# Two groups of four PSUM banks, and the next expert's transposes moved into the second layer

## The chip, the cores and the metric

The kernel runs on one core of one Trainium2 chip. The metric is the device time of one execution in microseconds (us). The median of three runs before the change is 928.09 us (925.41 to 928.22). TensorE (PE in the profile, PEld for its weight loads) multiplies matrices and writes its results to PSUM, a small memory of eight banks. VectorE (DVE) and ScalarE (ACT) read the results out of the banks; GpSimd (POOL) works on SBUF here, and SyncE (SP) issues most DMAs.

## The reference

Three pieces run one behind the other on 2304 tokens (4 batches of 576) of 512 values.

- Attention with 8 heads of 64, causal, with a window of 128 positions and a linear bias by distance.
- A mixture of eight experts: each token goes to the one expert with the largest gate logit, through `relu(x @ w1[e]) @ w2[e]` (512 to 1024 to 512), and is scaled by its gate probability times a sigmoid.
- A gated layer for all tokens: `silu(x @ w_gate) * (x @ w_val) @ w_out` (512 to 1536 to 512).

```python
for e in range(E):
    h = np.maximum(x[mask] @ w1[e], 0.0)
    out[mask] = gate_w[mask, None] * eom[mask, e, None] * (h @ w2[e])
silu = g * (1.0 / (1.0 + np.exp(-g)))
return (silu * val @ w_out)
```

## The kernel before, in words

**Stages.** Up to about 178 us the attention runs, whose order is written out by hand (`tc.manual_schedule`); it also scatters every token's row, already scaled, into the list of its expert in DRAM (`xs`). From 180 to 447 us the experts run, the fullest first. From 447 us the wide stage, the gated layer, takes the tokens in nine units of 256.

**The order of instructions.** Outside the attention the order on each engine is made by a planner when the kernel is built (`schedule_with_timeline_sim=True`). It goes by its own estimate of times; among instructions that it holds to be ready, those earlier in the program text go first. On the chip each engine then works off its fixed queue, and an instruction that waits holds up all that stand behind it.

**Numbers in two parts.** Every operand of a matmul is split into a high part and the rest that it leaves, and each product is made in three passes (`PASSES`): high by high, high by rest, rest by high. The high part is a copy by ScalarE, the rest a subtraction by VectorE or GpSimd.

**An expert** (loop over `p`) has `caps[p]` rows: 384, 384, 352, 336, 304, 272, 256, 256.

- `load_x(p)` loads its rows from DRAM by a DMA on SP's queue into the only buffer `xr`; `emit_xT(p)` turns them: for each of four blocks of 128 columns, TensorE transposes the rows into a bank `tx` (L907), ScalarE copies it to `xh` (L908) and VectorE makes `xl` (L909).
- First layer: eight groups `m` of 12 matmuls, each into one bank `oh` (L959). ScalarE makes `hh` (relu, L967), VectorE `hl` (L971); with `hl` the bank is free. After each group `w_step(2)` (L972) converts two blocks of weights of later stages.
- Then `emit_xT(p + 1)` and `load_x(p + 2)` (L976, L977).
- Second layer: four banks `oy` are held together. Its eight steps `kk` each take one eighth of the hidden values, `hh[kk]` and `hl[kk]`, into all four banks, 12 matmuls a step (L985). At the end ScalarE copies the banks to `y` (L998) and sends them to DRAM.

**A unit of the wide stage** (loop over `u`) makes 12 groups `m` of 24 matmuls, each into one bank `gv` that holds the gate and the value half (L1019). ScalarE takes the sigmoid (`sg`, L1028), VectorE multiplies (L1029) and makes `av` (L1030), after which the bank is free; ScalarE and VectorE (in unit 0 GpSimd) split `av` into `hh` and `hl`. Then two banks `oo` take the 72 output matmuls (L1043). The weights of this stage come as 64-bit numbers and are narrowed to fp32 by `narrow` (L276 on ScalarE, L277, L278 and L281 on VectorE) before they are split (L328, L329). A third of them is narrowed during the middle experts, the rest from about 406 us to 486 us, beside the last expert and the first unit.

**PSUM before.** All of these results, and the two of the preparation (`cnt_ps`, `warm`), take their banks from one pool of eight under one name, `"m"`, so that the banks go round in the order of the text:

```python
ps_m = wctx.enter_context(tc.tile_pool(name="ps_m", reuse_waits="tile", bufs=8, space=PSUM))
```

For an expert the round is eight `oh`, four `tx`, four `oy`: sixteen, twice all banks. So the four `tx` take the banks of the first four `oh`, the four `oy` those of the last four `oh`, and four of the next expert's eight `oh` those of the `oy`. In the wide stage `gv` of group m takes the bank that `gv` of group m-8 had, but for the two banks that go to `oo` in between.

Of the kernel before, what the change touches and what calls it, by code (L numbers as in the profile page):

```python
# [7 lines left out]
F32 = mybir.dt.float32  # L8
# [10 lines left out]
PSUM = bass.MemoryType.PSUM  # L19
# [7 lines left out]
def attn_moe_glu_kernel(ctx, tc, q, k, v, w_gate, w_ogate, w1, w2, w2_gate, w2_val, w2_out, out, caps=CAPS):  # L27
# [62 lines left out]
    with ExitStack():  # L90
# [35 lines left out]
            load_rows(j - 1, ("vr",))  # L126


        def keep_warm(pool, tag, n):
            o = pool.tile([128, 512], F32, tag=tag, name="warm")  # L130
            for _ in range(n):
                nc.tensor.matmul(out=o, lhsT=ones, rhs=ones.unsqueeze(1).to_broadcast([128, 4, 128]))

# [1 line left out]
        table = ac.tile([128, 1], F32, name="table")  # L135
        nc.scalar.activation(out=table, in_=ones[:, 0:1], func=AF.Exp)
        last_exp = [None]
        keep_warm(ps_t, "t", 12)
        nc.gpsimd.memset(ident, 1.0)
        nc.gpsimd.affine_select(  # L140
            out=ident, in_=ident, pattern=[[-1, 128]], compare_op=ALU.is_equal, fill=0.0, base=0, channel_multiplier=1
# [587 lines left out]
        ht_p = wctx.enter_context(tc.tile_pool(name="ht", reuse_waits="tile", bufs=1))  # L729
        s_p = wctx.enter_context(tc.tile_pool(name="sp", reuse_waits="tile", bufs=2))  # L730
        tb_p = wctx.enter_context(tc.tile_pool(name="tb", reuse_waits="tile", bufs=1))
        ps_m = wctx.enter_context(tc.tile_pool(name="ps_m", reuse_waits="tile", bufs=8, space=PSUM))

        nov = const.tile([128, 1], I32, name="nov")
        oid = const.tile([128, NBLK, 1], I32, name="oid")
        off_reg = [0] * E

        def tb(name, shape, dt=F32):
            return tb_p.tile([128] + shape, dt, tag=name, name=name)
# [10 lines left out]

        def expert_tables():

            cnt_ps = ps_m.tile([128, E], F32, tag="m", name="cnt_ps")
            for i in range(NGR):
                nc.tensor.matmul(out=cnt_ps, lhsT=ones, rhs=gs[:, i, :], start=(i == 0), stop=(i == NGR - 1))
            nc.vector.tensor_copy(cnt[:, 0, :], cnt_ps)
            key, srt = tb("key", [E]), tb("srt", [E])
            STT(out=key, in0=cnt[:, 0, :], scalar=float(E), in1=ktab, op0=ALU.mult, op1=ALU.add)
            nc.vector.max(out=srt, in_=key)
            ki, ci = tb("ki", [E], I32), tb("ci", [E], I32)  # L760
            nc.vector.tensor_copy(ki, srt)
            TS(out=reg[:, 0, :], in0=ki, scalar1=E - 1, scalar2=E - 1, op0=ALU.bitwise_and, op1=ALU.bitwise_xor)
            for p in range(1, E):
                e_reg[p] = nc.sync.value_load(reg[0:1, 0, p:p + 1], min_val=0, max_val=E - 1)
            TS(out=ci, in0=ki, scalar1=(1 << 15) - 1, scalar2=3, op0=ALU.bitwise_and, op1=ALU.logical_shift_right)
            held, end, off, ep = (tb(nm, [1, E]) for nm in ("held", "end", "off", "ep"))
            nc.vector.tensor_copy(ep[:, 0, :], reg[:, 0, :])
            nc.vector.tensor_copy(held[:, 0, :], ci)
            TT(out=held, in0=held, in1=capt, op=ALU.min)
            nc.vector.tensor_copy(end[:, :, 0:1], held[:, :, 0:1])  # L770
            for p in range(1, E):
                TT(out=end[:, :, p:p + 1], in0=end[:, :, p - 1:p], in1=held[:, :, p:p + 1], op=ALU.add)
            nc.vector.tensor_copy(total, end[:, :, E - 1:E])
            TT(out=off, in0=end, in1=held, op=ALU.subtract)
            nc.vector.tensor_copy(reg[:, 1, :], off[:, 0, :])

            own, pick = (t[:, 0:E, :] for t in scratch())
            TT(out=own, in0=iota8.unsqueeze(2).to_broadcast([128, E, E]), in1=ep.to_broadcast([128, E, E]),
               op=ALU.is_equal)
            for src, dst in ((off, offe), (capt, cape)):  # L780
                TT(out=pick, in0=own, in1=src.to_broadcast([128, E, E]), op=ALU.mult)
                RED(out=dst.rearrange("p a e -> p e a"), in_=pick, axis=AX, op=ALU.add)
# [95 lines left out]
        def pair_tile(pool, tag, w):  # L878
            return [pool.tile([128, w], F32R, tag=tag + x, name=tag + x) for x in "hl"]

        def grid(t, n, w):
            return t[:, 0:n * w].rearrange("p (k c) -> p k c", k=n)
# [11 lines left out]
            for x in placed:  # L894
                tc.add_manual_dep(r, x.name, DATA, reason="all tokens are placed")

        def emit_xT(p):
            if p >= E:
                return
            n = caps[p]  # L900
            cb = -(-n // 128)
            r = xr.pop(p)
            xh, xl = (grid(t, KD, n) for t in pair_tile(xe_p, "x", KD * cap))
            for kk in range(KD):
                t = ps_m.tile([128, CP], F32, tag="m", name="tx")
                for c in range(cb):
                    nc.tensor.transpose(t[:, c * 128:c * 128 + 128], r[:, c, kk * 128:kk * 128 + 128], ident)  # L907
                nc.scalar.activation(out=xh[:, kk, :], in_=t[:, 0:n], func=AF.Copy)  # L908
                TT(out=xl[:, kk, :], in0=t[:, 0:n], in1=xh[:, kk, :], op=ALU.subtract)  # L909
            xe[p] = (xh, xl)  # L910

        yr, x2 = {}, {}

# [23 lines left out]
        with tc.issue_after(last_exp[0]):  # L937
            nc.scalar.activation(out=tb("sig", [1]), in_=ident[:, 0:1], func=AF.Sigmoid)
        sorted_known[0] = True
        keep_warm(ps_m, "m", 30)  # L940
        emit_xT(0)
        while wn[0] < 8 or any(w[0][1] == 0 for w in loaded):
            w_step()
        load_x(1)
        for p in range(E):
# [6 lines left out]
                load_order()  # L952
            hh, hl = (grid(t, KF, n) for t in pair_tile(ht_p, "h", HW))
            for m in range(KF):
                o = ps_m.tile([128, cap], F32, tag="m", name="oh")
                i = 0
                for a, b in PASSES:
                    for kk in range(KD):
                        pace[0] = nc.tensor.matmul(  # L959
                            out=o[:, 0:n],  # L960
                            lhsT=wt["w1", p, m // 4, kk][:, a, (m % 4) * 128:(m % 4) * 128 + 128],
                            rhs=(xh, xl)[b][:, kk, :],
                            start=(i == 0),
                            stop=(i == 3 * KD - 1),
                        )
                        i += 1
                r = nc.scalar.activation(out=hh[:, m, :], in_=o[:, 0:n], func=AF.Relu).ins  # L967
                if p == 0 and m > 0:
                    with tc.issue_after(r):
                        off_reg[m] = nc.scalar.value_load(reg[0:1, 1, m:m + 1], min_val=0, max_val=NT)  # L970
                STT(out=hl[:, m, :], in0=o[:, 0:n], scalar=0.0, in1=hh[:, m, :], op0=ALU.max, op1=ALU.subtract)  # L971
                w_step(2)  # L972
                if m % 4 == 3:
                    freed[0] += 2
            if p + 1 < E:
                emit_xT(p + 1)  # L976
                load_x(p + 2)  # L977
            else:

                split_unit(0)  # L980
            o = [ps_m.tile([128, cap], F32, tag="m", name="oy") for _ in range(KD)]
            for kk in range(KF):
                for d in range(KD):
                    for i, (a, b) in enumerate(PASSES):
# [7 lines left out]
                if kk % 2:  # L992
                    freed[0] += 1
                    w_step(2)

            for d in range(KD):
                y = s_p.tile([128, CP], F32, tag="sc", name="y")[:, 0:n]
# [12 lines left out]
        for u in range(NU):  # L1010
            xh, xl = x2.pop(u)
            ah, al = (grid(t, KF2, 256) for t in pair_tile(ht_p, "h", HW))
            for m in range(KF2):
                gv = ps_m.tile([128, 2, 256], F32, tag="m", name="gv")
                for i, nm in enumerate(("g", "v")):
                    n = 0
                    for a, b in PASSES:
# [16 lines left out]
                    out=al[:, m, :], in0=av, in1=ah[:, m, :], op=ALU.subtract  # L1034
                )
            split_unit(u + 1)
            o = [ps_m.tile([128, DM], F32, tag="m", name="oo") for _ in range(2)]

            for kk, c in [(kk, c) for kk in range(KF2) for c in range(2)] if u < NU - 1 else [
                (kk, c) for c in range(2) for kk in range(KF2)  # L1040
# [141 lines left out]
```

## Time and profile before

| | us |
|---|---|
| median of three runs | 928.09 |
| profiled execution | 921.89 |
| its span | 920.0 |
| TensorE matmul busy (share of the span) | 850.5 (92%) |
| VectorE busy | 453.1 (49%) |
| ScalarE busy | 386.7 (42%) |
| GpSimd busy | 319.1 (35%) |

The span is the time from the first to the last instruction of the profiled execution; the 1.9 us around it belong to no instruction. Busy time is an average over stages with different limits: what a change in one stage is worth is read from the waits in that stage. A wait is put down to the engine and line that released it last. A row of the order of time begins with its start and its length; in brackets stands the idle time of the engine before it and what ended it. Matmuls are pipelined, so one is issued before the one ahead of it has ended, and the pace is read from start to start. [...]

### The profile page before, as it was taken

To read this page: it belongs to the slowest core of one execution; us is meant where nothing else is said; L and a number is where in the kernel's file an instruction comes from. 1 tells how busy PE (TensorE), PEld (TensorE's weight loads), DVE (VectorE), ACT (ScalarE), POOL (GpSimd) and SP (SyncE) were. 2 spreads that over 40 slices of the span, in tenths; PEclk is the share of its full clock that TensorE was granted. 3 is DMA by queue.
4 is the path that set the end of the run, shared out by engine and by line. 5 is a ranking of instruction groups with operands and counts; after the bars stand their busy time and mean duration, and the time that the engine had idled before them with its cause. 6 is when DMAs were issued, how large, how long until landed. Compare 5 with 4: busy or idle time off the path is not lost.

```text
span 920.0 us, 17155 instructions
## 1 busy us (share of the span) xinstructions
PE 850.5 (92%) x6291; PEld 781.3 (85%) x6291; DVE 453.1 (49%) x1292; ACT 386.7 (42%) x1046; POOL 319.1 (35%) x395
## 2 busy tenths in 40 slices
PE   7995987599699989998989999999999999999995
PEld 5784765399599989998988989999898989899994
DVE  6774899582454563249994423324141424233240
ACT  6894875152455656566663212223121212122220
POOL 4673876343156788775563000000000000000000
PEclk9997999889899999999999999999999999999998
DMA  9999521579766677666650101010100001010000
GB/s 186 206 297 256 151 70 40 171 169 130 209 200 203 205 232 241 208 187 201 199 175 2 46 1 46 1 47 1 47 1 27 20 1 47 1 47 1 25 1 25
DMA packets 105370, 99.36 MB, mean 108 GB/s; under 512 B 62786, under 2 KB 71490, under 8 KB 105282
## 3 DMA queue, kind: packets, MB, share of 16 engines
q1 hardware_dynamic: 95952, 83.47, 34.7%
q0 software_dynamic: 3520, 9.50, 2.8%
q10 hardware_dynamic: 5810, 5.25, 1.7%
q8 instruction: 51, 0.84, 0.4%
q14 instruction: 37, 0.30, 0.1%
HBM read 77.16 MB, written 21.04 MB: 107 GB/s over the span
## 4 chain that ended last, share of the span: by engine, by line
issue 29%; PE 28%; DVE 4%; POOL 2%; DMA 1%; ACT 0%; POOLq 0%; DVEq 0%; ACTq 0%
PE gv L1019 12%; PE oo L1043 7%; PE oy L985 5%; PE oh L959 4%; DVE rawd L277 1%; DVE rawd L278 1%; POOL out_dram L1053 1%; DVE rawd L281 1%; POOL w L329 1%; DMA ys<-y 0%; DMA rawd<-in_moe_w_gate_dram 0%; DMA rawd<-in_moe_w_val_dram 0%; POOL hl L1033 0%; PE tx L907 0%; DVE hl L971 0%
## 5 line engine op out<-in xcount | busy, mean ns | idle before, releaser
L1053 POOL DMA_INDIRECT out_dram<-xr,oid x18 | 17.3, 962 | 398.6 <-ACT xr L1052 388.7
L1029 DVE TENSOR_TENSOR sg<-gv,sg 128x256 f32<-128x256 f32 x108 | 45.8, 424 | 222.7 <-ACT sg L1028 222.7
L1043 PE MATMUL oo<-w,hh 128*128 128x512 f32 x432 | 137.8, 396 | 0.9 <-DVE av L1030 0.9
L1019 PE MATMUL gv<-xh,w 128*128 128x256 f32 x864 | 126.6, 281 | 3.3 <-DVE av L1030 3.3
L985 PE MATMUL oy<-hh,w 128*128 128x384 f32 (+5 forms) x512 | 119.0, 319 | 11.2 <-DVE hl L971 11.1
L1019 PE MATMUL gv<-xh,wx 128*128 128x256 f32 x864 | 125.0, 279 | 0.0
L1019 PEld LDWEIGHTS gv<-xh,w 128*128 128x128 f32 x864 | 112.9, 189 | 3.8 <-DVE av L1030 3.8
L1019 PEld LDWEIGHTS gv<-xh,wx 128*128 128x128 f32 x864 | 112.4, 188 | 0.7
L323 POOL TENSOR_TENSOR w<-raw,w 128x512 fp32r<-128x512 f32 x80 | 103.7, 1323 | 26.0 <-ACT w L321 14.5
L985 PEld LDWEIGHTS oy<-hh,w 128*128 128x128 f32 x512 | 89.6, 196 | 13.6 <-DVE hl L971 13.6
L321 ACT ACTIVATE w<-raw 128x512 fp32r<-128x512 f32 x128 | 74.5, 624 | 58.7 <-DMA raw<-in_moe_w_dram 39.4
L1043 PEld LDWEIGHTS oo<-w,hh 128*128 128x128 f32 x432 | 81.3, 188 | 20.5 <-DVE av L1030 1.3
L959 PE MATMUL oh<-xh,w 128*128 128x384 f32 (+5 forms) x512 | 91.5, 318 | 7.0 <-ACT y L998 5.5
L1028 ACT ACTIVATE sg<-gv 128x256 f32<-128x256 f32 x108 | 41.3, 382 | 112.2 <-PE gv L1019 111.9
L959 PEld LDWEIGHTS oh<-xh,w 128*128 128x128 f32 x512 | 81.3, 195 | 8.0 <-ACT y L998 6.0
L1043 PE MATMUL oo<-w,hl 128*128 128x512 f32 x216 | 85.4, 396 | 0.0
L1031 ACT ACTIVATE hh<-av 128x256 fp32r<-128x256 f32 x108 | 45.1, 418 | 92.6 <-DVE av L1030 92.4
L985 PE MATMUL oy<-hl,w 128*128 128x384 f32 (+5 forms) x256 | 81.0, 317 | 0.0
L1019 PE MATMUL gv<-xl,w 128*128 128x256 f32 x432 | 68.7, 281 | 0.0
L1019 PE MATMUL gv<-xl,wx 128*128 128x256 f32 x432 | 68.3, 279 | 0.0
L1033 DVE TENSOR_TENSOR hl<-av,hh 128x256 fp32r<-128x256 f32 x98 | 41.6, 425 | 44.1 <-ACT hh L1031 44.1
L1052 ACT ACTIVATE xr<-oo 128x512 f32<-128x512 f32 x18 | 10.8, 598 | 120.1 <-PE oo L1043 119.3
(201 smaller groups left out, 1478.7 us busy)
## 6 DMA issues: line engine op xcount, KB each, us to landing
raw<-in_moe_w_dram SPq DMA_DIRECT2D x128, 256.0 KB, 3.5
xs<-zrow SPq DMA_DIRECT2D x8, 774.0 KB, 7.2
rawd<-in_moe_w_gate_dram SPq DMA_DIRECT2D x24, 256.0 KB, 3.1
rawd<-in_moe_w_val_dram SPq DMA_DIRECT2D x24, 256.0 KB, 2.9
rawd<-in_moe_w_out_dram SPq DMA_DIRECT2D x24, 256.0 KB, 3.1
xr<-xs SPq DMA_DIRECT2D x6, 774.0 KB, 6.5
xr<-ys SPq DMA_DIRECT2D x9, 512.0 KB, 3.8
qr<-in_q_dram SPq DMA_DIRECT2D x16, 256.0 KB, 4.9
```

Source lines behind the costliest of these rows:

```text
L321: nc.scalar.activation(out=s[:, 0, :], in_=t, func=AF.Copy)
L323: low = lambda: eng.tensor_tensor(out=s[:, 1, :], in0=t, in1=s[:, 0, :], op=ALU.subtract)
L959: pace[0] = nc.tensor.matmul(out=o[:, 0:n], lhsT=wt["w1", p, m // 4, kk][:, a, (m % 4) * 128:(m % 4) * 128 + 128], rhs=(xh, xl)[b][:, kk, ...
L985: pace[0] = nc.tensor.matmul(out=o[d][:, 0:n], lhsT=wt["w2", p, 0, kk][:, a, d * 128:d * 128 + 128], rhs=(hh, hl)[b][:, kk, :], start=(kk ...
L1019: nc.tensor.matmul(out=gv[:, i, :], lhsT=wt[nm, -1, m // 4, kk][:, a, (m % 4) * 128:(m % 4) * 128 + 128], rhs=(xh, xl)[b][:, kk, :], start ...
L1028: nc.scalar.activation(out=sg, in_=gv[:, 0, :], func=AF.Sigmoid)
L1029: TT(out=sg, in0=gv[:, 0, :], in1=sg, op=ALU.mult)
L1031: nc.scalar.activation(out=ah[:, m, :], in_=av, func=AF.Copy)
L1033: (nc.gpsimd if u == 0 and m < 10 else nc.vector).tensor_tensor(out=al[:, m, :], in0=av, in1=ah[:, m, :], op=ALU.subtract)
L1043: nc.tensor.matmul(out=o[c], lhsT=(ah, al)[b][:, kk, c * 128:c * 128 + 128], rhs=wt["o", -1, 0, kk][:, a, :], start=(kk == 0 and i == 0), ...
L1052: nc.scalar.activation(out=ob[:, c, :], in_=o[c], func=AF.Copy)
L1053: r = nc.gpsimd.indirect_dma_start(out=out[:, :], out_offset=bass.IndirectOffsetOnAxis(ap=oid[:, 2 * u + c, :], axis=0), in_=ob[:, c, :], ...
```

## The change

The pool `ps_m` gets two names, `"oh"` and `"oy"`, of four buffers each, in place of one name of eight. To `"oh"` go the counts, the warm-up, the first layer, the transposes and `gv`; to `"oy"` the second layer, `oo` and the transposes of the first expert. `emit_xT(p + 1)` and `load_x(p + 2)` move from between the two layers to behind the first of the eight steps of the second layer (`kk == 0`). `keep_warm` gets its number of buffers as an argument; the number is the pool's own in both calls.

```diff
-        ps_m = wctx.enter_context(tc.tile_pool(name="ps_m", reuse_waits="tile", bufs=8, space=PSUM))
+        ps_m = wctx.enter_context(tc.tile_pool(name="ps_m", reuse_waits="tile", bufs=1, space=PSUM))
...
+        def bank(tag, w, name):
+            return ps_m.tile([128, w], F32, tag=tag, name=name, bufs=4)
...
-            cnt_ps = ps_m.tile([128, E], F32, tag="m", name="cnt_ps")
+            cnt_ps = bank("oh", E, "cnt_ps")
...
-        def emit_xT(p):
+        def emit_xT(p, tag="oh"):
...
-                t = ps_m.tile([128, CP], F32, tag="m", name="tx")
+                t = bank(tag, CP, "tx")
...
-        keep_warm(ps_m, "m", 30)
-        emit_xT(0)
+        keep_warm(ps_m, "oh", 30, 4)
+        emit_xT(0, "oy")
...
-                o = ps_m.tile([128, cap], F32, tag="m", name="oh")
+                o = bank("oh", cap, "oh")
...
-            if p + 1 < E:
-                emit_xT(p + 1)
-                load_x(p + 2)
-            else:
+            if p + 1 == E:
                 split_unit(0)
-            o = [ps_m.tile([128, cap], F32, tag="m", name="oy") for _ in range(KD)]
+            o = [bank("oy", cap, "oy") for _ in range(KD)]
             for kk in range(KF):
...
                 if kk % 2:
                     freed[0] += 1
                     w_step(2)
+                elif kk == 0:
+                    emit_xT(p + 1)
+                    load_x(p + 2)
...
-                gv = ps_m.tile([128, 2, 256], F32, tag="m", name="gv")
+                gv = bank("oh", 512, "gv").rearrange("p (a c) -> p a c", a=2)
...
-            o = [ps_m.tile([128, DM], F32, tag="m", name="oo") for _ in range(2)]
+            o = [bank("oy", DM, "oo") for _ in range(2)]
```

## Rows read from the trace of the kernel before

**Rows 1.** Page, part 1: busy us (share of the span) and instructions of each engine.
```profile
PE 850.5 (92%) x6291; PEld 781.3 (85%) x6291; DVE 453.1 (49%) x1292; ACT 386.7 (42%) x1046; POOL 319.1 (35%) x395
```

**Rows 2.** Waits of PE: line, released by, us in total, times, longest.
```profile
PE oy L985 <- DVE hl L971: 11.1, 8, 3.2
...
PE oh L959 <- ACT y L998: 5.5, 2, 4.5
...
PE gv L1019 <- DVE av L1030: 3.3, 2, 3.1
```

**Rows 3.** Windows: stretch, length, busy PE, PEld, DVE, ACT, POOL, PEclk, DMA, GB/s.
```profile
523.00:862.00 339.00, 339.00 (x2386) 316.13 (x2385) 107.64 (x242) 77.57 (x177) 13.41 (x14) 1.00 0.06 20
...
432.00:440.00 8.00, 5.86 (x34) 5.66 (x35) 8.00 (x21) 5.00 (x14) 4.14 (x5) 0.79 0.66 218
...
465.00:475.00 10.00, 10.00 (x86) 9.85 (x84) 10.00 (x24) 6.04 (x17) 6.28 (x8) 1.00 0.70 230
475.00:486.00 11.00, 7.65 (x50) 7.39 (x50) 10.55 (x23) 6.00 (x17) 8.28 (x11) 0.85 0.16 48
```

**Rows 4.** Order of time on PE, wide unit 0: start us, length us, instruction, wait.
```profile
446.63 0.63 PE L1019 MATMUL gv<-xh,wx 128*128 128x256 f32 x4
447.10 0.63 PE L1019 MATMUL gv<-xl,wx 128*128 128x256 f32 x4
...
481.50 0.74 PE L1019 MATMUL gv<-xh,w 128*128 128x256 f32 x4 [3.15 <-DVE av L1030]
...
485.80 0.59 PE L1043 MATMUL oo<-w,hh 128*128 128x512 f32 x1
...
503.94 0.28 PE L1019 MATMUL gv<-xh,wx 128*128 128x256 f32 x1
```

**Rows 5.** Order of time on DVE, wide unit 0: the first six `av`.
```profile
465.00 0.41 DVE L1030 TENSOR_TENSOR av<-gv,sg 128x256 f32<-128x256 f32 x1
...
469.41 0.41 DVE L1030 TENSOR_TENSOR av<-gv,sg 128x256 f32<-128x256 f32 x1
...
474.79 0.42 DVE L1030 TENSOR_TENSOR av<-gv,sg 128x256 f32<-128x256 f32 x1
...
481.04 0.41 DVE L1030 TENSOR_TENSOR av<-gv,sg 128x256 f32<-128x256 f32 x1
...
485.14 0.41 DVE L1030 TENSOR_TENSOR av<-gv,sg 128x256 f32<-128x256 f32 x1
...
487.25 0.43 DVE L1030 TENSOR_TENSOR av<-gv,sg 128x256 f32<-128x256 f32 x1 [0.52 <-POOL hl L1033]
```

**Rows 6.** Order of time on PE, experts 1 to 3.
```profile
221.48 0.86 PE L959 MATMUL oh<-xh,w 128*128 128x384 f32 x4
222.17 0.86 PE L959 MATMUL oh<-xl,w 128*128 128x384 f32 x4
...
238.61 1.65 PE L959 MATMUL oh<-xh,w 128*128 128x384 f32 x4 [4.48 <-ACT y L998]
...
270.93 0.81 PE L959 MATMUL oh<-xh,w 128*128 128x352 f32 x4
...
304.81 0.77 PE L959 MATMUL oh<-xh,w 128*128 128x336 f32 x4
305.42 0.78 PE L959 MATMUL oh<-xl,w 128*128 128x336 f32 x4
...
319.68 1.47 PE L907 MATMUL tx<-ident,xr 128*128 128x128 f32 x12
...
328.93 0.49 PE L985 MATMUL oy<-hh,w 128*128 128x336 f32 x1 [3.21 <-DVE hl L971]
```

**Rows 7.** Order of time on DVE: first `hl` of expert 1, first and last of expert 3.
```profile
242.13 0.55 DVE L971 SCALAR_TENSOR_TENSOR hl<-oh,hh 128x384 fp32r<-128x384 f32 x1
...
313.94 0.51 DVE L971 SCALAR_TENSOR_TENSOR hl<-oh,hh 128x336 fp32r<-128x336 f32 x1 [3.84 <-ACT hh L967]
...
328.38 0.49 DVE L971 SCALAR_TENSOR_TENSOR hl<-oh,hh 128x336 fp32r<-128x336 f32 x1
```

More of the change, by code (lines that the diff above doesn't have):

```diff
@@ L126, in attn_moe_glu_kernel, with keep_warm @@
             load_rows(j - 1, ("vr",))
-        def keep_warm(pool, tag, n):
-            o = pool.tile([128, 512], F32, tag=tag, name="warm")
+        def keep_warm(pool, tag, n, bufs):
+            o = pool.tile([128, 512], F32, tag=tag, name="warm", bufs=bufs)
             for _ in range(n):
@@ L137, in attn_moe_glu_kernel @@
         last_exp = [None]
-        keep_warm(ps_t, "t", 12)
+        keep_warm(ps_t, "t", 12, 3)
         nc.gpsimd.memset(ident, 1.0)
@@ L901, in emit_xT @@
             cb = -(-n // 128)
-            r = xr.pop(p)
-            xh, xl = (grid(t, KD, n) for t in pair_tile(xe_p, "x", KD * cap))
+            xe[p] = xh, xl = [grid(t, KD, n) for t in pair_tile(xe_p, "x", KD * cap)]
             for kk in range(KD):
-                t = ps_m.tile([128, CP], F32, tag="m", name="tx")
+                t = bank(tag, CP, "tx")
                 for c in range(cb):
-                    nc.tensor.transpose(t[:, c * 128:c * 128 + 128], r[:, c, kk * 128:kk * 128 + 128], ident)
+                    nc.tensor.transpose(
+                        t[:, c * 128:c * 128 + 128], xr[p][:, c, kk * 128:kk * 128 + 128], ident
+                    )
                 nc.scalar.activation(out=xh[:, kk, :], in_=t[:, 0:n], func=AF.Copy)
                 TT(out=xl[:, kk, :], in0=t[:, 0:n], in1=xh[:, kk, :], op=ALU.subtract)
-            xe[p] = (xh, xl)
         yr, x2 = {}, {}
```

## The prediction

> **What bounds the kernel now.** I read the busy shares first, then who TensorE waits for, then the stages by windows, and last the order of time around each wait. TensorE is busy for 850.5 of 920.0 us [rows 1], and from 523 to 862 us it is busy for 339.00 of 339.00 [rows 3]: units 1 to 7 of the wide stage are TensorE alone, and nothing that touches only the other engines can be seen there. What an edit can win or lose lies in the places where TensorE stands. In the two stages that the change touches these are four [rows 2]: the second layer of an expert (`oy`) waits 11.1 us in 8 places for the vector engine's `hl` (L971), the first layer (`oh`) 5.5 us for the copies of the results `y` (L998), the wide stage (`gv`) 3.3 us for `av` (L1030). So at most about 20 us can be removed, and the bank that a group of matmuls writes to is what ties it to these engines. The reader is to see in the windows that in unit 0 of the wide stage it is the vector engine that sets the pace: 10.00 of 10.00 us from 465 to 475, 10.55 of 11.00 from 475 to 486 [rows 3], because it still converts the last wide weights there (L277, L278, L281). Only there does TensorE run far ahead of those that empty its banks.
>
> **The change, part by part.** Instructions are the same in kind and number: the same transposes, copies, subtractions and DMAs; `keep_warm` gets the same three buffers as before. What changes is which bank each result takes, and where the transposes of the next expert stand. So every term is a wait.
>
> *Wide stage, unit 0: four banks for `gv` in place of eight.* Of today's eight banks the first group `gv0` starts at 446.63 and four matmuls take 0.47 us (446.63 to 447.10), so a group of 24 takes 2.82 [rows 4]. A bank is free when `av` has read it: `av0` ends at 465.00 + 0.41 = 465.41, `av1` at 469.82, `av2` at 475.21, `av3` at 481.45, `av4` at 485.55, `av5` at 487.68 [rows 5]. With eight banks TensorE meets this only at the eleventh and twelfth group: `gv11` starts at 481.50 after 3.15 us of waiting, when `av3` is through, and the output matmuls `oo` start at 485.80 [rows 4]. With four banks group m waits for `av` of m-4. If the vector engine keeps its order and pace, `gv4` starts at 465.4 instead of 446.63 + 4 x 2.82 = 457.9; `gv5` at 469.8, `gv6` at 475.2, `gv7` at 481.5, `gv8` at 485.6. From there TensorE is the slower one again (2.82 a group, while `av4` to `av5` is 2.1): `gv9`, `gv10`, `gv11` follow without a wait, and `oo` starts at 485.6 + 4 x 2.82 = 496.9. That is 11.1 us later than 485.80. Given back: `oo` today takes 503.94 - 485.80 = 18.1 us [rows 4] with some waiting in it for `av`; without it I take 1 us off (estimate; between 0 and 1.4). Term: +10 us. Its lower end is 0: if the evacuations stood earlier in the vector engine's queue, the conversions of the output weights, which `oo` needs only after 486, could wait. I take the upper value, since the queues are fixed when the kernel is built and an evacuation becomes ready only when its group is done, which four banks make no earlier. Queued behind a waiting `gv` are only more `gv` and `oo`; the vector engine has its conversions to do meanwhile. In the later units TensorE has no wait at all [rows 3], so four banks do as well as eight: 0.
>
> *First layer, four banks for `oh`.* The same rule: group m waits for `hl` of m-4. In expert 1 a group of 12 takes 3 x 0.69 = 2.08 us (221.48 to 222.17 for four), so the fifth would start at 221.48 + 8.3 = 229.8, while `hl0` ends at 242.13 + 0.55 = 242.68 [rows 6, 7]. Today TensorE stands from 234 to 238.61 for `y` [rows 6] and then three more times for `hl` at the second layer's banks. After, it stands once, 12.9 us, and does four groups from 242.7 to 251.0, or to 253 at the lower clock of the first ones; the second layer then finds free banks and runs its 8 x 2.08 = 16.6 us and the transposes' 1.5, to 269 or 271. Today expert 2 begins at 270.93 [rows 6]. Term: 0, between -2 and +2.
>
> *Second layer, banks of its own; transposes behind its first eighth.* Expert 3 shows the exchange best. `hl0` ends at 314.45 [rows 7], the fifth group of 1.86 us each (304.81 to 305.42 for four) would start at 312.25: +2.2. Today's first layer ends at 319.68, where the transposes start; after it ends at 314.45 + 4 x 1.86 = 321.9. Then the first eighth runs at once, since its banks are free, and the wait of 3.21 us at 328.93 [rows 6], which is for the bank of the last `hl` (328.38 + 0.49), goes from `oy` to the last of the four transposes, which now take the `oh` banks; by then two or three eighths are done. Today's 3.2 and the slow matmuls behind it go, 2.2 and a rest of the wait come: I take -2, between -3.5 and +1. Transposes, their 12 matmuls in some 1.5 us [rows 6], cost the same in either place. Behind them stand the copies `xh`, `xl` and SP's load of the rows of the expert after next; all are moved by one eighth, about 2 us, with seven eighths (13 us) left before the next first layer needs them. That cover hides them; it is gone only if the last `hl` is later than the whole second layer. SP's weight loads queued behind that row load would then wait too: up to +2 in an expert. Experts 2 and 7 have waits of the same sort of 1 to 2 us, which turn from one bank's wait into another's: 0, between -2 and +1. The other experts have hardly any wait now, 8 for `hl` and 2 for `y` in all [rows 2]: 0.
>
> The sum: +10 (unit 0) + 0 (expert 1) - 2 (expert 3) + 0 = +8 us. The profiled execution took 921.9 us, 920.0 of span and 1.9 around it; after, about 930. The runs shown (925.4 to 928.2, median 928.1) all lie above it, the median by 6 us; the difference is what carries over, so I add the 8 to the median: 936.
>
> [...]
>
> **Rivals.**
> 1. *The clock stays low through the bank waits.* Five waits in 30 us, and then `gv8` to `gv11` at 4.30 us instead of 2.82: 4 x 1.48 = +6 on top, 942. For it: the windows of 0.79 and 0.85. Against it: `gv8` hardly waits, since `gv7` ends when `av4` does. Chance 0.15.
> 2. *The queues come out in another order, and the bank waits of unit 0 vanish (faster).* The planner lays the queues anew. If it puts `av0` to `av4` some 10 us earlier among the conversions, term one is 0, and what is left is what the second layer wins: -2 by expert 3, up to -6 if experts 1, 2 and 7 keep a third of their waits off; taking the middle, 924. It decides from `av4` ending before 475. Against it: the vector engine is full up to 486, and its conversions come from weights that TensorE's progress frees, not from the banks. Chance 0.15.
> 3. *Both halves meet:* part of the evacuations move, unit 0 loses 2 to 4 us, the experts win as much; 928. That is also where a change that only renames banks would stand. Chance 0.15.
>
> **How the numbers follow.** The forecast has 0.55, with its own range of 931 to 940 (+3 to +12: the bounds of expert 1, expert 3 and of the give-back in `oo`). The range to hold the time 8 times in 10 takes in most of rivals 1 and 3 and leaves out half of rival 2: 926 to 943. What a measurement of this kernel can tell from no change is 0.3%, 2.8 us. Faster by more: 0.14 (rival 2, without its end near nothing). Within: 0.16 (rival 3 and the edge of rival 2). Slower: 0.70 (forecast and rival 1).
>
> **What would show it.** In the profile after: TensorE's waits of `gv` for `av` grow from 3.3 us to some 15, in about five places, the first near `gv4`; `oo` of unit 0 starts some 8 to 11 us later, counted from `gv0`. `oy` for `hl` falls from 11.1 to under 4, some of it back under the transposes (`tx`); `oh` for `y` is replaced by one wait of over 10 us for `hl` in expert 1. Units 1 to 7 keep their length to 0.1%. The prediction is wrong if `gv` does not wait more than now, or if the stage of the experts gains over 6 us.

## The result and the profile after

The changed kernel takes 935.7 us, the median of four runs (931.6 to 939.9); the kernel before took 927.5 in four runs beside them (925.4 to 928.2). By the medians that is 8.2 us slower. The ratio of the runs is 1.0102 with a 95% interval of 1.0061 to 1.0143, or 9.5 us slower, between 5.7 and 13.3. The forecast was 936. The profiled execution took 933.1 us, its span 931.1, against 921.9 and 920.0.

Busy time is nearly what it was [rows 1], so the time went into waits:

```profile
PE 852.7 (92%) x6291; PEld 782.5 (84%) x6291; DVE 460.6 (49%) x1292; ACT 386.6 (42%) x1046; POOL 320.8 (34%) x395
```

The waits of TensorE after the change (released by, us in total, times, longest). The 11.1 us of `oy` for `hl` [rows 2] are gone; `oh` and the transposes `tx` wait for `hl` instead, and `gv` waits 9.0 us where it waited 3.3:

```profile
PE oh L963 <- DVE hl L975: 10.5, 3, 8.5
PE gv L1023 <- DVE av L1034: 9.0, 3, 6.4
...
PE tx L910 <- DVE hl L975: 4.9, 2, 2.5
PE oy L986 <- ACT hh L971: 4.3, 1, 4.3
```

Unit 0 of the wide stage in TensorE's order of time, to set against [rows 4]. Read the starts: the first four groups take 2.82 us each, `gv4` waits 6.40 us (468.20) for `av0`, two later groups wait less. From 488.42, where `gv8` begins, four groups take 11.3 us without a wait, so each is at its full pace. Eight of the 72 matmuls of `oo` stand in the gaps from 480.10 on; the other 64 begin at 499.74, and unit 1 at 514.68:

```profile
450.34 0.63 PE L1023 MATMUL gv<-xh,wx 128*128 128x256 f32 x4
...
468.20 1.22 PE L1023 MATMUL gv<-xh,wx 128*128 128x256 f32 x4 [6.40 <-DVE av L1034]
...
473.39 0.63 PE L1023 MATMUL gv<-xh,wx 128*128 128x256 f32 x4
...
477.17 0.74 PE L1023 MATMUL gv<-xh,wx 128*128 128x256 f32 x4 [0.79 <-DVE av L1034]
...
480.10 0.40 PE L1047 MATMUL oo<-w,hh 128*128 128x512 f32 x1
...
483.02 0.85 PE L1023 MATMUL gv<-xh,wx 128*128 128x256 f32 x4 [1.82 <-DVE av L1034]
...
488.42 0.66 PE L1023 MATMUL gv<-xh,w 128*128 128x256 f32 x4
...
499.74 0.63 PE L1047 MATMUL oo<-w,hh 128*128 128x512 f32 x2
...
514.68 0.28 PE L1023 MATMUL gv<-xh,wx 128*128 128x256 f32 x1
```

The first and the fifth `av` of that unit on the vector engine. They lie 17.4 and 37.5 us behind `gv0`; before it was 18.4 and 38.5 [rows 4, 5]. All of the first five end 1.0 to 2.2 us earlier than before by this count. So the evacuations (the reads that empty the banks) kept about their place and pace:

```profile
467.74 0.41 DVE L1034 TENSOR_TENSOR av<-gv,sg 128x256 f32<-128x256 f32 x1
...
487.86 0.41 DVE L1034 TENSOR_TENSOR av<-gv,sg 128x256 f32<-128x256 f32 x1
```

Windows (length; busy PE, PEld, DVE, ACT, POOL; PEclk, DMA, GB/s). PEclk is the mean clock that was granted to TensorE, as a share of full speed. The first begins with the transfers of the last 48 wide-weight chunks (a chunk is the block of 128x256 weights that is narrowed and split at a time), in expert 6, and ends with the last copy of one (L328): the vector engine is idle for 7.1 of 85.0 us. The last is units 1 to 7, TensorE alone as in [rows 3]; each of these units takes 50.72 us in both kernels:

```profile
403.87:488.90 85.03, 69.44 (x521) 67.43 (x521) 77.94 (x170) 48.55 (x135) 53.55 (x57) 0.90 0.58 177
459.00:468.00 9.00, 2.80 (x24) 2.60 (x23) 9.00 (x19) 5.27 (x15) 5.45 (x7) 0.91 0.84 239
468.00:475.00 7.00, 6.80 (x38) 6.80 (x39) 7.00 (x15) 4.36 (x13) 4.77 (x6) 0.63 0.64 220
565.00:918.00 353.00, 353.00 (x2513) 330.06 (x2512) 113.86 (x258) 81.84 (x189) 14.37 (x15) 1.00 0.06 21
```

The same stretch before (both begin 9 us behind expert 6's first `oh`) has 2.6 us of idle time in 81.7:

```profile
403.56:485.30 81.74, 75.14 (x603) 73.85 (x603) 79.14 (x170) 49.27 (x133) 51.48 (x57) 0.96 0.60 183
```

What makes the vector engine idle can be seen on GpSimd. A group of the second half-copies of the wide weights (L329), its duration in ns (least, median, most), from expert 6 to the end of unit 0, first before and then after:

```profile
L329 POOL TENSOR_TENSOR w<-rawd,w x48: 739/872/1798, 412.9 to 485.8; 128x256 fp32r<-128x256 f32 x48
```

```profile
L329 POOL TENSOR_TENSOR w<-rawd,w x48: 737/834/3874, 413.6 to 490.1; 128x256 fp32r<-128x256 f32 x48
```

After the change one copy lasts 3.87 us, and while it lasts the vector engine works through its conversions without a gap, at 0.28 and 0.42 us each. The buffers that this copy and the four behind it hold come free late, the transfers into them start late (the longest wait of a transfer for such a copy, from 405 to 430 us, grows from 2.2 to 5.5 us), and the vector engine stands for 3.32 us. SP's waits for these copies (in total, times, longest), before and after; then GpSimd's row, and the vector engine's last rows of that run and the first after the gap:

```profile
SPq L302 <- POOL w L329: 9.8, 11, 2.2
```

```profile
SPq L302 <- POOL w L329: 11.0, 9, 5.5
```

```profile
417.42 3.87 POOL L329 TENSOR_TENSOR w<-rawd,w 128x256 fp32r<-128x256 f32 x1 [2.05 <-ACT w L328]
```

```profile
419.73 0.29 DVE L277 TENSOR_SCALAR rawd<-rawd 128x256 int32<-128x256 int32 x1
419.93 0.75 DVE L278 SCALAR_TENSOR_TENSOR rawd<-rawd 128x256 int32<-128x256 int32 x2
424.01 0.30 DVE L277 TENSOR_SCALAR rawd<-rawd 128x256 int32<-128x256 int32 x1 [3.32 <-DMA rawd<-in_moe_w_gate_dram]
```

### The profile page after: what moved, and what is told of

The parts are those of the page before. It is cut to its first block, busy times and chain, and to the rows that moved or that the text cites. A ratio compares the mean times of both kernels' runs of the same rounds, so it can differ in the third digit from the quotient of the medians.

```text
span 931.1 us, 17143 instructions
## 1 busy us (share of the span) xinstructions
PE 852.7 (92%) x6291; PEld 782.5 (84%) x6291; DVE 460.6 (49%) x1292; ACT 386.6 (42%) x1046; POOL 320.8 (34%) x395
## 4 chain that ended last, share of the span: by engine, by line
PE 36%; issue 32%; DMA 9%; DVE 8%; POOL 8%; ACT 5%; SPq 1%; POOLq 0%; DVEq 0%; ACTq 0%
PE gv L1023 13%; PE oo L1047 7%; PE oh L963 6%; PE oy L986 4%; DMA raw<-in_moe_w_dram 4%; POOL w L323 3%; DMA rawd<-in_moe_w_gate_dram 2%; PE s L360 2%; DMA rawd<-in_moe_w_val_dram 2%; ACT p L402 1%; PE o L451 1%; DVE w L323 1%; POOL w L329 1%; PE tq L344 1%; POOL out_dram L1057 1%
## 5 line engine op out<-in xcount | busy, mean ns | idle before, releaser
L1023 PE MATMUL gv<-xh,wx 128*128 128x256 f32 x864 | 127.1, 282 | 9.0 <-DVE av L1034 9.0
L1023 PEld LDWEIGHTS gv<-xh,wx 128*128 128x128 f32 x864 | 113.7, 190 | 10.6 <-DVE av L1034 9.9
L986 PE MATMUL oy<-hh,w 128*128 128x384 f32 (+5 forms) x512 | 116.8, 313 | 5.1 <-ACT hh L971 4.3
L963 PE MATMUL oh<-xh,w 128*128 128x384 f32 (+5 forms) x512 | 93.4, 321 | 13.0 <-DVE hl L975 10.5
L321 ACT ACTIVATE w<-raw 128x512 fp32r<-128x512 f32 x128 | 76.1, 627 | 64.1 <-DMA raw<-in_moe_w_dram 39.7
L986 PEld LDWEIGHTS oy<-hh,w 128*128 128x128 f32 x512 | 87.1, 191 | 5.8 <-ACT hh L971 4.5
```

The lines of the kernel that those rows point to most:

```text
L321: nc.scalar.activation(out=s[:, 0, :], in_=t, func=AF.Copy)
L963: pace[0] = nc.tensor.matmul(out=o[:, 0:n], lhsT=wt["w1", p, m // 4, kk][:, a, (m % 4) * 128:(m % 4) * 128 + 128], rhs=(xh, xl)[b][:, kk, ...
L986: pace[0] = nc.tensor.matmul(out=o[d][:, 0:n], lhsT=wt["w2", p, 0, kk][:, a, d * 128:d * 128 + 128], rhs=(hh, hl)[b][:, kk, :], start=(kk ...
L1023: nc.tensor.matmul(out=gv[:, i, :], lhsT=wt[nm, -1, m // 4, kk][:, a, (m % 4) * 128:(m % 4) * 128 + 128], rhs=(xh, xl)[b][:, kk, :], start ...
```

## The experiments

One table carries them. It cuts each profile at four points: A, the first `oh` of expert 6; B, the last L328 copy of a wide weight; C, the first `gv` of unit 1; and the end. From C to the end it is 416.1 to 416.5 us in every kernel of the table. A itself scatters by 10 us between executions of the same queues, so the stretches are compared and not the profiles' totals. The stretches scatter too: e2 and e10 have the same queues from A on, and differ by 3.3 us from A to `gv0` and by 1.3 from A to C. In e6, e7, e9 and e12 the last copy stands later by design, so only A to C can be compared there. Ratios are to the kernel before on the same chip; "long copies" are GpSimd copies of 128x256 over 2 us near there.

| kernel | median us | ratio (95%) | A to gv0 | A to B | B to C | A to C | long copies |
|---|---|---|---|---|---|---|---|
| before | 927.5 | | 52.1 | 90.7 | 18.7 | 109.4 | none |
| after | 935.7 | 1.0102 (1.0061–1.0143) | 55.5 | 94.0 | 25.8 | 119.8 | 3.87 |
| e1 banks alone | 936.9 | 1.0075 (1.0048–1.0103) | 53.5 | 92.7 | 25.3 | 118.0 | 4.01 |
| e2 move alone | 930.9 | 1.0028 (1.0010–1.0046) | 55.6 | 96.1 | 18.7 | 114.7 | 3.89, 2.47 |
| e3 gv in turn | 935.6 | 1.0062 (1.0041–1.0084) | 56.7 | 93.7 | 24.1 | 117.8 | 3.88 |
| e4 and expert 7 | 935.3 | 1.0062 (1.0043–1.0081) | 57.8 | 94.8 | 23.7 | 118.6 | 3.88 |
| e5 gv in rounds | 931.4 | 1.0027 (1.0006–1.0047) | 55.7 | 93.8 | 19.5 | 113.2 | 3.88 |
| e6 chunks behind av | 925.5 | 0.9949 (0.9931–0.9967) | 52.0 | 98.6 | 9.0 | 107.6 | none |
| e7 e5 and e6 | 926.9 | 0.9967 (0.9953–0.9980) | 55.5 | 98.8 | 9.1 | 107.9 | 3.88 |
| e8 shift only | 916.8 | 0.9853 (0.9826–0.9881) | 48.1 | 66.9 | 39.7 | 106.6 | none |
| e9 last rows back | 925.8 | 0.9976 (0.9957–0.9996) | 54.8 | 100.0 | 9.1 | 109.1 | 4.01 |
| e10 last rows alone | 931.0 | 1.0024 (1.0004–1.0043) | 52.3 | 94.7 | 18.7 | 113.4 | 3.88, 2.47 |
| e12 four banks, e6 | 935.1 | 1.0087 (1.0072–1.0102) | 55.2 | 98.6 | 16.6 | 115.2 | 3.88 |

So the profiled 11.1 us between before and after are: +0.3 up to A, +3.3 from A to B, +7.1 from B to C, +0.4 behind C.

**e1, the banks alone.** The changed kernel with the transposes put back:

```
-            if p + 1 == E:
+            if p + 1 < E:
+                emit_xT(p + 1)
+                load_x(p + 2)
+            else:
                 split_unit(0)
...
-                elif kk == 0:
-                    emit_xT(p + 1)
-                    load_x(p + 2)
```

> Only the bank half of the change: two groups of four, with the transposes back between the two layers. Theory T (the time goes to the wait for a bank wherever the vector engine lags: 7.0 us in unit 0 of the wide stage, 3.4 us in expert 7): 8 to 11 us above the kernel before, within 2 us of the changed kernel; unit 0 from its first gv to unit 1's first gv takes 63 to 65 us against 57.3 before. Rival R (the transposes in their new place move the order of the queues, and that costs it): within 3 us of the kernel before, unit 0 at 57 to 59 us.

Measured: +7.0 us (4.5 to 9.6 by the interval), unit 0 in 64.5 us. Theory T holds for unit 0; the move isn't needed for most of the loss. Of T's 3.4 us in expert 7 only 1.4 show (A to `gv0`).

**e2, the move alone.** The kernel before with its eight banks, and `emit_xT(p + 1)`, `load_x(p + 2)` behind `kk == 0`.

> Only the other half: eight banks under one tag as before, the next expert's transposes behind kk = 0 of the second layer. Theory T: within 2 us of the kernel before, unit 0 at 57 to 58 us; in the experts the first-layer tiles of the next expert now take banks that the second layer's results left last, so a wait of 2 to 5 us before the first layer of one or two experts can stand in the trace and make it up to 4 us slower. Rival R: at least 6 of the changed kernel's 8 us appear here.

Measured: +2.6 us (0.9 to 4.3), B to C 18.7 as before. The two halves, 7.0 and 2.6, make 9.6; the whole, 8.2, has that in its interval. That is above T's 2 us, within the 4 that it allowed for waits in the experts, and far from R's 6. Unit 0's length came out at 59.1, above what T said: its first five `av` ended 1.0 to 1.9 us later behind `gv0`, and there were two long copies (3.89 and 2.47 us) on GpSimd.

**e3, gv over both groups in turn.**

```
-                gv = bank("oh", 512, "gv")...
+                gv = bank(("oh", "oy")[m % 2], 512, "gv")...
```

> The changed kernel, with the wide stage's gv tiles taken from the two groups in turn, so that eight are open again; experts as changed. Theory T: unit 0 back to 57 to 58.5 us from 64.35, the total 6 to 7 us under the changed kernel (929 to 930 by medians), expert 7's 3 us stay. Rival R (the order of the queues, not the number of open banks): within 2 us of the changed kernel, unit 0 above 62 us.

Measured: 935.6 us, 5.8 above the kernel before (3.8 to 7.8), B to C 24.1 against the changed kernel's 25.8, unit 0 in 61.1. T as I had put it, eight open banks are enough, is wrong: no `gv` waits for an `av` any more, but `oo` does. The rows of TensorE:

```profile
496.02 0.76 PE L1047 MATMUL oo<-w,hh 128*128 128x512 f32 x1 [4.31 <-DVE av L1034]
...
499.35 0.79 PE L1047 MATMUL oo<-w,hh 128*128 128x512 f32 x1 [1.71 <-DVE av L1034]
```

With the groups in turn the two `oo` tiles take the banks of `gv5` and `gv7`, in the kernel before those of `gv4` and `gv5`. Behind the wait the clock is low too (0.57 in this window):

```profile
496.00:507.00 11.00, 9.27 (x24) 6.84 (x25) 6.29 (x14) 5.40 (x14) 3.75 (x6) 0.57 0.00 1
```

**e4, expert 7's `oh` in turn as well** (`bank("oy" if p == E - 1 and m % 2 else "oh", ...)`).

> As the kernel with eight open gv tiles, and expert 7's first-layer tiles also taken from the two groups in turn. Theory T: the wide stage begins at 446 to 448 us again instead of 450.3 and the total is 9 to 11 us under the changed kernel by the profiles, so within 2 us of the kernel before. A second explanation for expert 7 (its conversions were late because a transfer of wide weights was issued 1.7 us later, with 4.3 us of gap on the vector and scalar engines near 424 us, not because of banks): the wide stage still begins at 449 to 451 us and the total stays within 1 us of the kernel with eight gv tiles alone.

Measured: as e3 (935.3 and 935.6), and A to `gv0` is 57.8. More banks for `oh` in expert 7 give nothing, so its 3.4 us are not a matter of how many `oh` has. That leaves the late transfers, which e9 and e10 test.

**e5, gv in rounds of eight.** `bank("oh" if m % 8 < 4 else "oy", ...)`, so that every tile of unit 0 meets the same `av` as with one group of eight.

> The changed kernel with the wide stage's gv tiles in rounds of eight: m 0 to 3 and 8 to 11 from the first group, 4 to 7 from the second, so that the two oo tiles take the banks of gv4 and gv5, as in the kernel before (with the groups in turn they took those of gv5 and gv7, free at 495.9 and 499.3 us). Theory T2 (unit 0's part of the cost is which av each bank waits for): from the start of the last wide-weight copy on the scalar engine (L328) to unit 1's first gv it takes 18.6 to 19.5 us, as before and with the move alone (18.6 both), against 25.8 in the changed kernel and 24.1 with the groups in turn; total 929 to 932 us. What is left above the kernel before, 1 to 3 us, is the held copy on GpSimd (3.9 us near 420 us). Rival (any second group of banks costs it): still 24 to 26 us and a total of 935 to 937 us.

Measured: B to C 19.5 us, total +2.5 (0.6 to 4.4). Against the changed kernel's ratio that takes back 7 us with one line. Unit 0's term is which `av` a bank waits for. What is left is as large as the move alone.

**e6, the chunks of the output weights behind the `av`s**, on the kernel before. `tc.issue_after(r)` keeps what stands under it, as far as it runs on the engine of `r`, behind `r` in that engine's queue:

```
-        while wjobs or loaded:
+        while any(w[0][0] != "o" for w in wjobs + loaded):
             w_step()
+        w_step(4)
...
-                TT(out=av, in0=gv[:, 1, :], in1=sg, op=ALU.mult)
+                r = TT(out=av, in0=gv[:, 1, :], in1=sg, op=ALU.mult).ins
+                with tc.issue_after(r):
+                    w_step(2)
```

> The kernel before, with all but the first four chunks of the output weights converted behind unit 0's av's, two behind each, instead of ahead of them. Theory T2 (in unit 0 the vector engine is the bound, and which of its work comes first decides what TensorE waits for): av0 ends at about 452 to 456 us instead of 465, no gv waits, oo runs close behind the last chunk, and unit 1 begins 2 to 5 us earlier counted from gv0: unit 0 takes 52 to 56 us against 57.3; total 924 to 927 us by medians of the kernel before's 929. Rival (the vector engine's whole work bounds unit 0 whatever its order): unit 0 at 57 to 59 us, total within 1.5 us of the kernel before.

Measured: 925.5 us, 4.7 us under the kernel before (3.1 to 6.4), the fastest median here; unit 0 takes 55.6 and no `gv` waits. A to C is 107.6 against 109.4 (110.4 in e11, which has the kernel before's queues up to C). So 1.8 to 2.7 of the 4.7 us lie there; where the rest lies these profiles don't show. One step of T2 missed: `av0` was to end 5 to 9 us behind `gv0` and ended 17.4 behind it (before, 18.8). It is the next ones that came earlier: `av1` to `av5` end 20.4 to 35.5 us behind `gv0`, before 23.2 to 41.0.

**e7, e5 and e6 together** on the changed kernel.

> The changed kernel with both edits: gv tiles in rounds of eight, and the output weights' chunks behind the av's. Theory T2: as the kernel before with the chunks behind the av's, plus 1 to 3 us for the held copy on GpSimd: unit 0 at 52 to 56 us, total 925 to 930 us. Rival: at or above 930 us, unit 0 above 57 us.

Measured: 926.9 us, 3.1 under the kernel before (1.9 to 4.4). TensorE is busy for 51.57 of unit 0's 52.45 us. The intervals of e6, e7 and e9 overlap; which is fastest isn't settled:

```profile
453.06:505.51 52.45, 51.57 (x363) 47.12 (x361) 45.11 (x95) 27.64 (x76) 27.95 (x36) 1.00 0.40 121
```

**e8, two of the three vector operations of a conversion left out** (L278 and L281), on the changed kernel.

> The changed kernel with two of the vector engine's three operations on each of the 72 wide-weight chunks left out (the two that put the bits together; what it computes there is not the reference's). Theory T (four banks cost only where the vector engine lags behind TensorE): unit 0 takes 50.7 to 53 us and no gv waits over 1 us for an av; the total is 20 to 35 us under the changed kernel. Rival (four banks, or the order of the queues, cost by themselves): unit 0 stays above 57 us, with waits of gv.

Measured: 916.8 us, 13.7 under the kernel before and so some 20 under the changed one, but unit 0 takes 58.5 us, and `gv4` still waits:

```profile
457.73 1.22 PE L1017 MATMUL gv<-xh,wx 128*128 128x256 f32 x4 [6.08 <-DVE av L1028]
```

Theory T's 50.7 to 53 us without waits are refuted, and the rival's signs came: over 57 us, with waits of `gv`. The rival left open whether banks or the order of the queues cost it; the trace points to the order. The vector engine isn't full there; from 440 to 458 us it waits 13 times for transfers, at the shift of the next chunk, and `av0` stands behind those shifts in its queue:

```profile
DVE rawd L277 <- DMA rawd<-in_moe_w_out_dram: 7.1, 13, 1.5
```

So the lag that four banks are too few for is one of place in the queue and not only of load. That is also what e6 uses. No GpSimd copy of 128x256 over 2 us stands here, where the vector engine's runs are thin (those 13 waits make 7.1 us).

**e9, the last expert's transposes alone put back**, on e7 (`elif kk == 0 and p + 2 != E`, and the old place for `p + 2 == E`).

> The changed kernel with gv in rounds of eight and the output weights' chunks behind the av's, and with the transposes of the last expert alone put back between the layers of expert 6. Theory T3 (expert 7's 3.4 us come from the last expert's transposes in their new place: the vector engine then runs without a stop near 418 us, a GpSimd copy lasts 3.9 us instead of 0.9, and the transfers and copies behind it are late): no GpSimd copy over 2 us between 410 and 430 us, and from expert 6's first oh to the wide stage's first gv it takes 52 to 53.5 us instead of 55.5; if the vector engine's chain is the bound, unit 1 begins 105 to 106.5 us after expert 6's first oh instead of 107.9, total 924 to 926 us. Rival (all moves of the transposes together, or the groups of banks in expert 7): still 55 to 56 us, a total as with the last rows moved, 926 to 928.

Measured: 925.8 us, and no long copy near 420, as T3 says; but one of 4.01 us at 456, as e1 has at 453, and A to C 109.1, no better than e7. A to `gv0` is 54.8 and expert 7 itself takes 31.3 us, near the rival's, though TensorE's two long waits in it (3.39 and 2.43 us) end 17 to 20 us before that copy begins. So the long copy near 420 isn't what lengthens expert 7 here.

**e10, the last expert's transposes alone moved**, on the kernel before.

> The kernel before with one thing changed: the transposes of the last expert, and of it alone, behind kk = 0 of expert 6's second layer. Theory T3: a GpSimd copy of 3.5 to 4 us near 420 us, and 55 to 56 us from expert 6's first oh to the first gv instead of 52.1; unit 1 begins 112.5 to 114.7 us after expert 6's first oh instead of 109.4; total 2 to 4 us above the kernel before. Rival: 52 to 53 us, no long copy, and a total within 1 us of the kernel before.

Measured: +2.2 us (0.4 to 4.0), A to C 113.4, and the copy:

```profile
420.53 3.88 POOL L329 TENSOR_TENSOR w<-rawd,w 128x256 fp32r<-128x256 f32 x1 [2.25 <-ACT w L328]
```

This one move brings the long copy and about the loss of the whole move. Not as expected is where it shows: A to `gv0` stayed at 52.3, and the time is lost in unit 0 (61.1 us). e2 has the same queues from A on and the same two long copies, and there A to `gv0` is 55.6 and unit 0 59.1. What mainly tells the two apart is TensorE's clock (0.58 against 1.00) behind the last bank wait of expert 7, which is 1.60 us long in e2 and 1.59 in e10. The window of 6 us behind it, e2 first, has 34 matmuls against 50:

```profile
440.00:446.00 6.00, 6.00 (x34) 6.00 (x33) 5.64 (x15) 3.90 (x11) 2.55 (x3) 0.58 0.84 301
```

```profile
440.00:446.00 6.00, 5.97 (x50) 5.97 (x51) 5.46 (x13) 3.14 (x9) 2.82 (x4) 1.00 0.91 303
```

Why the clock fell in one and not in the other is open. So the same queues can lose the time in expert 7 or in unit 0. The vector engine's chain is late either way (A to B 96.1 and 94.7 us, before 90.7).

**e11, rows of vector instructions beside a GpSimd copy**, behind the last unit of the kernel before; the core of it:

```
+                for j in range(n):                  # n = 12, then 36
+                    d = f if j == 1 else s[j % 12]
+                    (tensor_scalar if j % 3 == 0 else scalar_tensor_tensor of two inputs) -> d
+                for p in (p0, p1):
+                    nc.gpsimd.tensor_tensor(out=p, in0=f, in1=g, op=subtract)
```

> The kernel before with a measurement behind its last unit: on the vector engine 12 and then 36 instructions in a row, of the conversion's two kinds (0.28 and 0.42 us each by the traces, on data of no use) with nothing to wait for, and on GpSimd two copies of 128x256 that come free at the second instruction of each row; then one GpSimd copy with the vector engine idle. Theory H (GpSimd does not get in between two of the vector engine's instructions that follow without a gap, so a copy lasts as long as the row does): the first copy of each row lasts 3 to 4.5 us and 11 to 14 us, the second 0.7 to 0.9 us, the one alone 0.7 to 0.8 us, and the row's instructions keep 0.28 and 0.42 us. Rival (they take turns, an instruction each): no copy over 1.5 us in either row, and two or three instructions of each row at 0.8 to 1.0 us; the 3.9 us copies near 420 us then have another cause.

Measured, GpSimd's first copy in the row of 12, in the row of 36, and the one with the vector engine idle:

```profile
923.28 0.75 POOL L1081 TENSOR_TENSOR mbq<-mbf,mbg 128x256 f32<-128x256 f32 x1 [0.60 <-DVE mbf L1077]
```

```profile
927.74 10.45 POOL L1081 TENSOR_TENSOR mbq<-mbf,mbg 128x256 f32<-128x256 f32 x1 [2.98 <-DVE mbf L1077]
...
939.28 0.73 POOL L1083 TENSOR_TENSOR mbq<-mbf,mbg 128x256 f32<-128x256 f32 x1 [0.41 <-DVE mbf L1082]
```

The row of 36 is as theory H says: the copy came free at 927.74, while the third instruction ran, and ended at 938.19; the last of the other 33 ended at 937.60. The row of 12 is as the rival says: the copy got in, and vector instructions beside it are long, where a row that keeps its pace has 0.28 and 0.41:

```profile
923.03 0.41 DVE L1077 SCALAR_TENSOR_TENSOR mbs<-mba,mbb 128x256 int32<-128x256 int32 x1
923.36 0.82 DVE L1075 TENSOR_SCALAR mbs<-mba 128x256 int32<-128x256 int32 x1
924.10 1.28 DVE L1077 SCALAR_TENSOR_TENSOR mbs<-mba,mbb 128x256 int32<-128x256 int32 x2
```

Both happened. In the row of 36 the copy was held until the row was through, 10.45 us, and what decides between the two is open. Up to the measurement this kernel has the queues of the kernel before, and its profile gives 52.2 us from A to `gv0`, 91.7 from A to B and 18.7 from B to C: here the stretches repeat to 1 us.

**e12, e6's order with four banks**, on the changed kernel.

> The changed kernel with the output weights' chunks behind the av's, two behind each, and gv left in the first group of four. Theory T2: by the kernel with gv in rounds of eight and the same order (gv4 at gv0 + 11.3, av0's end at gv0 + 14.4, then an av every 3.8 us), gv4 waits 3 us and each later gv 1 us more, so that gv11 begins with av7's end at about gv0 + 40 instead of gv0 + 31, and TensorE fills part of the waits with oo: unit 0 takes 55 to 60 us against 52.4, total 929 to 933 us, above the rounds of eight by 2 to 6. Rival (with the av's early four banks are enough, and the order alone was at fault): unit 0 at 52 to 54 us, total 925 to 928 us.

Measured: 935.1 us, 8.1 above the kernel before (6.7 to 9.5) and above the expected total; unit 0 takes 60.0. The steps are right: `gv4` waits 2.98 us, and `gv11` begins 40.3 us behind `gv0`:

```profile
470.70 0.74 PE L1023 MATMUL gv<-xh,wx 128*128 128x256 f32 x4 [2.98 <-DVE av L1034]
...
496.54 0.74 PE L1023 MATMUL gv<-xh,w 128*128 128x256 f32 x4 [0.47 <-DVE av L1034]
```

Not right is that `oo` would fill the waits: all of it ran behind `gv11`. In this order too four banks cost 7 us against the rounds of eight (A to C, 115.2 and 107.9).

## Why the prediction came out

By its steps, each with what was measured. An expert's length is from its first `oh` to the next one's; it is a mean over the profiles with the same queues there: four of the kernel before's (before, e6, e10, e11) and seven of the changed kernel's (after, e3, e4, e5, e7, e9, e12); for expert 7, where e4, e9 and e10 differ, without these.

- **Unit 0, +10: right in mechanism, +7.0 in size** (from `gv0` to unit 1, 57.31 to 64.35 us). `gv4` to `gv8` were to start 18.8, 23.2, 28.6, 34.9 and 39.0 us behind `gv0`; they started 17.9, 23.1, 26.8, 32.7 and 38.1 behind it. The bulk of `oo` starts 10.2 us later counted from `gv0` (forecast 11.1). Mis-sized is the give-back, taken as 1 us: `oo` from there takes 14.9 us instead of 18.1. About 1.2 of these 3.2 us are its waits, as forecast (without waits the 72 matmuls take 50.72 - 12 x 2.82 = 16.9 us, by a later unit); the rest are the eight of the 72 that were laid into the bank waits. The waits of `gv` came to 9.0 us in three places, where the forecast had some 15 in about five: a slow `gv4` stands in place of the wait before `gv5`, and four matmuls of `oo` run just ahead of `gv8`. That "queued behind a waiting `gv` are only more `gv` and `oo`" was true; that some of this `oo` stood ahead of it I hadn't seen.
- **Expert 7, 0: wrong, +3.6** (28.6 to 32.2). The step that failed is the costing of the moved transposes by their own work and their cover only. They also lay the vector engine's queue anew; a GpSimd copy is held for 3.9 us, and A to B grows by 3.3. That this copy lengthens expert 7 isn't shown: e9 has a long expert 7 without it, e10 a short one (28.8) with it. In the profile after, TensorE's waits there are 4.34, 0.80 and 1.44 us where 0.97, 1.02 and 1.17 stood, and the clock is 0.78 and 0.77 in the stretches 425 to 432 and 432 to 440 us, before 1.00 and 0.79. In e2 the low clock behind one wait (0.58, in e10 1.00) cost expert 7 some 2 us, most of which unit 0 gave back; that is an estimate from the 34 matmuls against 50 in 6 us, 0.12 us each. How the 3.6 us divide among queue, banks and clock stays open.
- **Expert 2, 0: wrong by the means, +3.2** (34.3 to 37.5; single profiles 33.7 to 35.8 and 34.8 to 38.8). The wait did not turn into one as long: TensorE stands for `hl` ahead of the fourth transpose for 2.0 to 3.9 us, where it stood 1.45 to 1.93 in the second layer, and behind the longest of these waits the clock is low (0.57 over 6.60 us). TensorE's row in e5, and the window behind it; in the profile after the wait is 2.52 us and the clock stays at 1.00:

```profile
292.37 0.90 PE L910 MATMUL tx<-ident,xr 128*128 128x128 f32 x3 [3.93 <-DVE hl L975]
```

```profile
292.40:299.00 6.60, 6.60 (x26) 6.60 (x27) 3.01 (x8) 2.13 (x5) 2.74 (x3) 0.57 0.67 204
```

- **Expert 3, -2: -2.1 by the means** (36.8 to 34.7), but the single profiles overlap (34.1 to 38.7 and 32.6 to 37.1), and experts 2 and 3 go against each other from profile to profile: e5 has 38.8 and 32.8, e3 36.1 and 37.1, and e10, with the kernel before's queues, 35.8 and 34.1. Together they are 1.1 us longer, so the gain forecast here isn't shown. **Expert 1, 0: -2.0** (51.9 to 49.9), at the edge of its bounds; its waits became one of 8.5 us for `hl` in the profile after and 10.3 to 15.1 in the others. Experts 1 to 5 together give -0.4 by these means, and single sums scatter from 171.9 to 179.5, so this sum is not told from nothing.
- **The sum, +8: measured +8.2 by the medians**, which is in part luck, because misses cancel. By terms of the profiles: -0.4 (experts 1 to 5), +3.6 (expert 7), +7.0 (unit 0), +0.4 (behind it) make +10.6; the forecast had -2, 0, +10, 0. (The text before the sum speaks of four places where TensorE stands and names three; their 19.9 us are all that it counts.)
- **Rival 1, the clock:** the clock did fall behind the bank waits (0.63 from 468 to 475 us, where `gv4` takes 5.2 us instead of 2.8). It made `gv5` begin 1.0 us behind the end of `av1`, but `gv6` had to wait for `av2` anyway, and `gv8` to `gv11` kept 2.8 us where this rival has 4.30 (485.80 - 481.50 in [rows 4]), so its +6 did not come. Elsewhere low clock behind a wait did cost: in expert 2 (0.57 in e5), in e3 behind the wait of `oo` (0.57), and in expert 7 (0.58 in e2 against 1.00 in e10), for which the forecast had no such term.
- **Rivals 2 and 3, evacuations moved:** refuted, `av0` to `av4` ended 1.0 to 2.2 us earlier counted from `gv0` and not some 10. That their place decides is right all the same: with it changed by hand the kernel before wins 4.7 us (e6), and the changed kernel with rounds of eight some 5 (e5 and e7, 931.4 and 926.9).

## To carry to other kernels

Splitting the ring of PSUM banks cost nothing here while the engine that empties it kept up (units 1 to 7, 50.72 us each in both kernels). Where it lagged, in unit 0, the four banks that `gv` lost made `oo` start 10.2 us later, nearly four groups of 2.82, and 3.2 of that came back; that is one place and no rule. Count for every tile, the consumer's too, which evacuation its bank waits for (e3 against e5). Where a lag sits, look at the order of the evacuating engine's queue too: e6's order alone won 4.7 us on the kernel before, though with four banks the same order won next to nothing (e12, ratio 1.0087, where the changed kernel has 1.0102). An edit that only moves instructions still lays the other queues anew, and on engines that run full that can cost as much as the edit was to win (e10, +2.2 us).

## What the hardware showed unexpectedly

A GpSimd subtraction of 128x256 that takes 0.73 us with the vector engine idle (e11) took 3.87 to 4.01 us in ten of these kernels and 10.45 us in e11. In the profile after and in e11 the vector engine ran integer operations on SBUF (the memory that holds all these operands) without a gap meanwhile, and the copy ended 0.61 us (421.29 against 420.68) and 0.59 us (938.19 against 937.60) behind the last of them, which fits a copy that does nearly all its work after them. Where the two take turns, in e11's row of 12 and in the kernel before from 414.9 to 422.4 us, the copy takes 0.75 to 0.94 us and a vector operation beside it 0.82 to 0.97 instead of 0.28 and 0.42. So in these traces each of the two engines holds the other up, but not always by single instructions: a copy that waits for one vector instruction waits 0.28 or 0.42 us, and in e11 it waited through 33. Which orders bring this about is open: three profiles with the kernel before's queues up to unit 0 (before, e6, e11) show no copy of the weights over 2 us, the ten kernels with other queues that convert in full show one of 3.87 to 4.01 us each, two of them (e2, e10) a second of 2.47, and e8, with the vector engine's runs thinned, none.
